# Landmarks loaded onto 128 partitions, a casting load ahead of the identity, and a written-out order for every engine

## The chip, the cores and the metric

The kernel runs on one core of a Trainium2 chip. The metric is the device time of one execution in microseconds. Before the change the median of three runs is 244.42 us (243.48 to 244.64).

## The reference

Eight batches of landmark attention with eight heads are followed by a two-layer network with a smooth ReLU. Each head has 576 tokens of 64 elements and 32 landmarks `p`; the network takes 4608 tokens of 512 elements through 2048 hidden ones.

```python
def sm_attn(qq, kk, vv):
    s = scale * np.matmul(qq, kk.transpose(0, 1, 3, 2))
    a = np.exp(s - np.max(s, axis=-1, keepdims=True))
    a = a / (np.sum(a, axis=-1, keepdims=True) + 1e-09)
    return np.matmul(a, vv)
p_packed = sm_attn(p, k, v)
out = sm_attn(q, p_packed, p_packed)          # 8 x 8 x 576 x 64
x = out.transpose(0, 2, 1, 3).reshape(4608, 512)
h = x @ w_in                                  # 512 x 2048
g = np.where(h >= 1, h, np.where(h <= -1, 0, (h + 1) ** 2 / 4))
return g @ w_out                              # 2048 x 512
```

## The kernel before

**Per batch.** The keys and queries are turned so that the head's 64 elements lie on partitions: by TensorE (PE) for batches 0 and 1 (`tp`, L471), by transposing transfers on SyncE's queue (SP) for the others (L500). The scores of landmarks against keys (`sp`, L528) go through ScalarE's (ACT) exponential (`ex`, L533); their product with the values is `pk` (L624, L619), cast into `ppT`. The scores of queries against landmarks (`s`, L700) give `eT` (L723); its sums (`sm`, L728), their logarithm and its negative exponential (`ln`, `rc`) and one product on VectorE (DVE) give `A` (L742). The values meet `w_in` first: `mp` (L686) is `ppT` times a quarter of `w_in`, cast into `M` (L271). The hidden layer is then `h` = `M` times `A` (L814), in 16 pieces of 128 hidden elements. Each piece goes through `x` on ACT (L820), `t` on DVE or ACT (L828, L830) and a product into `hT` on DVE (L835). The second layer takes 16 products per 128 tokens into `o` (L889); `o` is copied to `ob` and stored.

**Landmarks.** `pT` holds them turned, `[64 twice, batch, g, a, x, 32]`. Before, `p_raw` and `p_nat` hold the landmark number on 32 partitions, two batches loaded by one transfer each on SP's and ACT's queues (L395); the rest (`p_late`) by six casting loads of GpSimd (L375). PE turns them against the identity (L426, L421) and four copies per group write `pT`.

**Loads.** GpSimd (POOL) issues the casting loads, float32 to bfloat16, in one queue: k, v and q of batch 0, the quarters of `w_in` and `w_out`, and then batch after batch (`load`, `load_w_in`, `load_w_out`). Half of batch 0's keys comes as float32 over SP's and ACT's queues into `k_raw` (L401) and is cast by DVE and ACT.

**What sets the order.** Every step is a `Task` with its engines, costs, dependences and buffers. `Plan.run` is a list scheduler with a model of the two kinds of queues: at each moment it takes the ready step that can start first, by a rank where several can. The ranks come from the table `AT`, `HID`, `OUT` (two numbers per batch and stage). Steps are emitted in the order of their starts, so each engine's queue is in that order. The gaps that the plan leaves on PE before the first `o` are filled with products of a tile of zeros (`warm`, L942). Where a step may run on DVE or ACT, the plan chooses.

```python
w, o, kT, x, t, ob = 3, 2, 2, 4, 4, 4      # buffers that matter; w and o are in PSUM
LOADS = "k0 v0 q0 win0 win1 wout0 k1 win2 win3 wout1 v1 wout2 q1 wout3 v2 q2 p k2"
```

Of the kernel before, what the change touches and what calls it, by code (L numbers as in the profile page):

```python
# [11 lines left out]
class Task:  # L12
# [4 lines left out]
    def __init__(self, rank, ways, deps=(), takes=(), mode=None, behind=()):  # L17
        self.rank, self.ways, self.deps = rank, ways, list(deps)
        self.behind = [d for d in behind if d is not None]
        self.takes, self.frees, self.mode = list(takes), [], mode  # L20
        self.start = self.end = self.engine = None
        self.users = []


class Plan:
# [8 lines left out]
    CLAIM = 0.3  # L34
# [4 lines left out]
    def __init__(self, buffers):  # L39
# [8 lines left out]
    def add(self, rank, ways, deps=(), takes=(), mode=None, behind=()):  # L48
        t = Task(rank, ways, deps, takes, mode, behind)
        self.tasks.append(t)  # L50
        return t
# [38 lines left out]
    def run(self, slack):  # L90
# [7 lines left out]
        ready = [t for t in self.tasks if not waiting[id(t)]]  # L98
        done = []

        def served(users):
            for u in users:
                waiting[id(u)] -= 1
                if waiting[id(u)] == 0:
                    ready.append(u)

        def finished(t):
# [5 lines left out]
            served(t.users)  # L113

        while len(done) < len(self.tasks):
            best = None
            found = defaultdict(list)
            left = {b: sorted(v) for b, v in self.slots.items()}
            for t in sorted(ready, key=lambda t: t.rank):
                at = max((d.end + self.LATENCY for d in t.deps), default=0.0)  # L120
                at = max([at] + [d.start + 0.001 for d in t.behind])
                need = defaultdict(int)
                for b in t.takes:
                    need[b] += 1
                short = any(len(left[b]) < n for b, n in need.items())
                wants = at < self.free["PE"] + self.CLAIM
                for b, n in need.items():
                    if not short:
                        at = max(at, left[b][n - 1] + self.LATENCY)
                    if wants:  # L130
                        del left[b][:n]
                if short:
                    continue
                for e in t.ways:
                    if e == "SP" and self.held is not None:
                        continue
                    start = max(self.free[e], at)
                    if e == "PE" and self.mode is not None and t.mode != self.mode:
                        start = max(start, self.free[e] + self.SWITCH)
                    found[e].append((start, t))  # L140
            for e, some in found.items():
                first = min(x[0] for x in some)
                at, t = min((x for x in some if x[0] <= first + slack.get(e, 0.0)), key=lambda x: (x[1].rank, x[0]))
                if best is None or at < best[0]:
                    best = at, t, e
# [5 lines left out]
            assert best is not None, "no step can take its buffers"  # L151
            at, t, e = best
            if e == "PE" and t.mode != self.mode:
                at = max(at, self.free[e] + self.SWITCH)
            ready.remove(t)
            keep, lasts = t.ways[e][:2]
            t.start, t.engine, t.end = at, e, at + lasts
# [6 lines left out]
            served(started[id(t)])  # L164
# [19 lines left out]
def kernel(  # L184
# [20 lines left out]
    P = 128  # L205
# [17 lines left out]
    SPLIT, AHALF, WPARTS, MPARTS, QLATE, ORDER3, ORDER = 2, 1, 1, 0, 1, 0, 2  # L223
# [3 lines left out]
    L1 = 15.967  # L227
    AT = [dict(kT=148.161, qT=275.48, sc=149.063, pk=-49.085, s2=-3.905, sm=-182.602, M=178.569, **{"M+": -129.863}),
          dict(kT=-39.644, qT=-48.123, sc=-66.351, pk=124.743, s2=170.079, sm=-187.478, M=-105.149, **{"M+": 146.812}),
          dict(kT=115.732, qT=51.477, sc=130.42, pk=237.931, s2=-181.084, sm=-29.758, M=169.369, **{"M+": -44.412}),  # L230
          dict(kT=29.446, qT=-25.092, sc=52.472, pk=243.839, s2=179.754, sm=-32.11, M=115.586, **{"M+": -71.343}),
          dict(kT=38.536, qT=86.402, sc=153.04, pk=258.796, s2=-13.152, sm=-43.327, M=-95.344, **{"M+": 110.184}),
          dict(kT=1.864, qT=113.754, sc=282.551, pk=400.409, s2=-26.009, sm=-92.874, M=125.845, **{"M+": 0.958}),
          dict(kT=126.633, qT=239.492, sc=-4.526, pk=382.024, s2=-90.437, sm=32.434, M=177.14, **{"M+": -62.453}),
          dict(kT=27.261, qT=148.76, sc=40.741, pk=216.362, s2=-45.985, sm=130.271, M=1.019, **{"M+": -201.613})]
    HID = [(27.4, 1.3921), (-10.054, 2.601), (22.49, 3.9747), (126.895, 4.8485), (231.121, 9.6612), (-18.141, 4.6461), (3.622, 15.8949), (451.41, 5.8147)]
    OUT = [[(235.954, -183.0), (268.544, -106.533), (35.947, 20.528), (122.624, -48.891)],
# [24 lines left out]
    plan = Plan(dict(BUFS, dma=8, exn=1))  # L262
# [28 lines left out]
    p_raw = work.tile([NP, 2, H, D], f32, tag="vv", name="p_raw", bufs=BUFS["vv"])  # L291
    p_nat = work.tile([NP, 2, H, D], bf16, tag="ln", name="p_nat", bufs=BUFS["ln"])
# [22 lines left out]
    consts = plan.add(-1000, {"DVE": (2.4, 2.4, constants)})  # L315

    identity = plan.add(-998.5, {"POOL": (0.6, 1.25, lambda e: make_identity(nc, ident))})
# [3 lines left out]
    last_of = {"loads": identity}  # L321
# [8 lines left out]
    def dma(key, rank, emit, mb, takes=(), settle=0.9):  # L330
        t = plan.add(rank, {"DMA": (0.78, 2.1, emit, mb / 0.405, settle)}, takes=list(takes) + ["dma"])
        plan.release("dma", [t])
        chain("loads", t)
# [14 lines left out]
    def load(nm, b, rank):  # L348
# [629 lines left out]
```

## Time and profile before

| | us |
|---|---|
| median of three runs | 244.42 (243.48 to 244.64) |
| span of the profiled execution, first to last instruction | 241.1 |
| median less span | 3.3 |
| PE busy | 233.3 |
| ACT busy | 192.7 |
| DVE busy | 177.6 |
| POOL busy | 31.4 |
| granted TensorE clock, mean | 1.000 |

The profiled execution has no time of its own beside its span; the median of the runs stands for it. One row of a profile's group or timeline names the line, engine, operation and tiles (written <- read), then a count and times. Times in the timeline count from the span's start. "Idle" is the time in which the engine stood before an instruction, with what ended it in brackets.

### The profile page before, as it was taken

To read this page: it belongs to the slowest core of one execution; us is meant where nothing else is said; L and a number is where in the kernel's file an instruction comes from. 1 tells how busy PE (TensorE), PEld (TensorE's weight loads), DVE (VectorE), ACT (ScalarE), POOL (GpSimd) and SP (SyncE) were. 2 spreads that over 40 slices of the span, in tenths; PEclk is the share of its full clock that TensorE was granted. 3 is DMA by queue.
4 is the path that set the end of the run, shared out by engine and by line. 5 is a ranking of instruction groups with operands and counts; after the bars stand their busy time and mean duration, and the time that the engine had idled before them with its cause. 6 is when DMAs were issued, how large, how long until landed. Compare 5 with 4: busy or idle time off the path is not lost.

```text
span 241.1 us, 5370 instructions
## 1 busy us (share of the span) xinstructions
PE 233.3 (97%) x2117; PEld 133.9 (56%) x2154; DVE 177.6 (74%) x311; ACT 192.7 (80%) x342; POOL 31.4 (13%) x47
## 2 busy tenths in 40 slices
PE   8999999999999999999999999999999999999995
PEld 2646555466554665466645564465546644565454
DVE  4549997678967998789936898689999955899000
ACT  3779996988969985999776988999789988888111
POOL 8462006200220040030030003000000000000000
PEclk9999999999999999999999999999999999999999
DMA  7999999996999999999999999999930301202233
GB/s 158 196 206 207 206 205 205 197 241 132 125 198 149 234 164 251 152 221 221 194 165 246 233 141 147 161 141 226 191 94 4 85 5 44 71 21 65 65 87 90
DMA packets 64138, 37.03 MB, mean 154 GB/s; under 512 B 36720, under 2 KB 59632, under 8 KB 64112
## 3 DMA queue, kind: packets, MB, share of 16 engines
q0 software_dynamic: 24336, 18.25, 52.6%
q1 hardware_dynamic: 38960, 17.87, 36.7%
q10 hardware_dynamic: 816, 0.56, 0.8%
q8 instruction: 17, 0.28, 0.5%
q14 instruction: 9, 0.07, 0.1%
HBM read 37.22 MB, written 9.44 MB: 194 GB/s over the span
## 4 chain that ended last, share of the span: by engine, by line
PE 81%; DVE 6%; DMA 5%; ACT 4%; POOL 2%; issue 2%; POOLq 0%; ACTq 0%
PE o L889 48%; PE h L814 21%; DMA w_in_sb<-in_moe_w_in_dram 5%; DVE hT L835 4%; PE mp L686 3%; PE pk L619 2%; PE sm L728 1%; DVE t L828 1%; ACT x L820 1%; PE sp L528 1%; PE s L700 1%; ACT t L830 1%; POOL q L352 1%; ACT M L271 1%; PE o L942 1%
## 5 line engine op out<-in xcount | busy, mean ns | idle before, releaser
L889 PE MATMUL o<-w_out_sb,hT 128*128 128x512 bf16 (+2 forms) x574 | 140.9, 367 | 1.9 <-issue 0.6
L835 DVE SCALAR_TENSOR_TENSOR hT<-t 128x576 bf16<-128x576 f32 (+1 forms) x130 | 93.7, 746 | 4.3 <-ACT t L830 2.3
L820 ACT ACTIVATE x<-h 128x576 f32<-128x576 f32 (+1 forms) x130 | 78.6, 651 | 9.1 <-PE h L814 8.5
L889 PEld LDWEIGHTS <-hT 128*128 128x128 bf16 x608 | 55.8, 98 | 49.8 <-issue 6.1
L814 PE MATMUL h<-A,M 128*128 128x288 bf16 x512 | 78.5, 286 | 0.6 <-ACT M L271 0.3
L814 PEld LDWEIGHTS <-M 128*128 128x128 bf16 x512 | 49.9, 98 | 27.6 <-issue 1.1
L830 ACT ACTIVATE t<-x 128x576 f32<-128x576 f32 (+1 forms) x57 | 39.4, 693 | 0.6
L828 DVE TENSOR_SCALAR t<-x 128x576 f32<-128x576 f32 (+1 forms) x73 | 33.3, 456 | 7.1 <-ACT x L820 6.7
L271 ACT COPY ob<-o 128x512 f32<-128x512 f32 (+2 forms) x22 | 12.0, 552 | 17.0 <-PE o L889 16.9
L742 DVE SCALAR_TENSOR_TENSOR A<-eT,rs,rc 128x576 bf16<-128x576 bf16 (+1 forms) x18 | 12.8, 748 | 11.5 <-ACT rc L737 11.5
L271 ACT CAST M<-mp 128x1024 bf16<-128x1024 f32 (+1 forms) x20 | 19.1, 992 | 2.7 <-PE mp L686 2.7
L352 POOL DMA_DIRECT2D k<-in_k_dram x8 | 6.7, 843 | 87.8 <-DMA kT<-k 68.4
L271 DVE CAST M<-mp 128x1024 bf16<-128x1024 f32 (+1 forms) x13 | 15.3, 1180 | 3.1 <-PE mp L686 3.1
L271 DVE COPY ob<-o 128x512 f32<-128x512 f32 x16 | 10.8, 688 | 6.9 <-PE o L889 6.9
L723 ACT ACTIVATE eT<-s,rs 128x576 bf16<-128x576 f32 x16 | 11.1, 742 | 2.5 <-PE s L700 2.5
L942 PE MATMUL o<-zeros 128*128 128x512 bf16 (+1 forms) x35 | 10.5, 431 | 1.3 <-DVE zeros L307 1.2
L732 ACT ACTIVATE ln<-sm 128x576 f32<-128x576 f32 x16 | 10.3, 652 | 1.2 <-PE sm L728 0.7
L686 PE MATMUL mp<-w_in_sb,ppT 64*32 64x512 bf16 x256 | 10.9, 380 | 0.2
L271 ACT CAST ppT<-pk 64x128 bf16<-64x128 f32 x24 | 6.2, 260 | 5.7 <-PE pk L634 4.0
L737 ACT ACTIVATE rc<-ln 128x576 f32<-128x576 f32 (+1 forms) x18 | 10.4, 625 | 0.1
L352 POOL DMA_DIRECT2D v<-in_v_dram x8 | 6.2, 779 | 21.9 <-PE pk L624 15.2
L533 ACT ACTIVATE ex<-sp 96x768 bf16<-96x768 f32 (+1 forms) x12 | 8.1, 709 | 0.5 <-PE sp L528 0.4
(59 smaller groups left out, 116.7 us busy)
## 6 DMA issues: line engine op xcount, KB each, us to landing
v<-in_v_dram POOLq DMA_DIRECT2D x8, 576.0 KB, 11.6
out_dram<-ob SPq DMA_DIRECT2D x23, 192.0 KB, 4.5
k<-in_k_dram POOLq DMA_DIRECT2D x7, 576.0 KB, 8.7
q<-in_q_dram POOLq DMA_DIRECT2D x7, 576.0 KB, 12.8
out_dram<-ob SPq DMA_DIRECT2D x24, 128.0 KB, 2.9
w_out_sb<-in_moe_w_out_dram POOLq DMA_DIRECT2D x4, 512.0 KB, 19.7
w_in_sb<-in_moe_w_in_dram POOLq DMA_DIRECT2D x3, 512.0 KB, 15.2
out_dram<-ob SPq DMA_DIRECT2D x23, 64.0 KB, 4.5
```

The costliest lines, as they stand in the source:

```text
L271: i = (nc.vector.tensor_copy if e == "DVE" else nc.scalar.copy)(to, of)
L352: G_.dma_start(tokens(nm, b)[:, heads(hs)], rows_of(nm, b, hs))
L686: m = nc.tensor.matmul(have["mp", b, f][a * NP:(a + 1) * NP, g], have["ppT", b][r, g, a], w_in_sb[r, a, f * FW:(f + 1) * FW], start=True, ...
L723: nc.scalar.activation(have["eT", b, g], have["s2", b, g][:, :, :HALF], AF.Exp, scale=rs_of[b][:, g, 1:])
L742: V.scalar_tensor_tensor(have["A", b][:, g, xs], have["eT", b, g][:, xs], rs_of[b][:, g, :1], have["rc", b, g][:, xs], ALU.mult, ALU.mult)
L814: nc.tensor.matmul(have["h", b, fi][:, hf, :HALF], have["M", b][:, g, fi * P:(fi + 1) * P], have["A", b][:, g, hf], start=(g == 0), stop=( ...
L820: nc.scalar.activation(have["x", b, fi][:, hs[0]:hs[-1] + 1], have["h", b, fi][:, hs[0]:hs[-1] + 1, :HALF], AF.Prelu, bias=-1.0, alpha=0.5)
L828: V.tensor_scalar(t, x, 1.0, 0.0, ALU.add, ALU.max)
L830: nc.scalar.activation(t, x, AF.Relu, bias=1.0)
L835: V.scalar_tensor_tensor(dst, t, 1.0, t, ALU.min, ALU.mult)
L889: nc.tensor.matmul(have["o", key][:, :w], hT[:, fi, i * P:(i + 1) * P], w_out_sb[:, fi, cols], start=(fi == 0), stop=(fi == KF - 1))
L942: nc.tensor.matmul(o[:, :w], zeros[:, :P], zeros[:, :w], start=True, stop=True)
```

## The change

The landmarks lie on 128 partitions: partition 16 h + m holds landmarks 2m and 2m + 1 of head h, 128 elements, so a row read from memory is 512 bytes instead of 256. Batches 0 and 1 come in one transfer on SP's queue (ACT's queue now starts with its half of `k_raw`), batches 2 to 7 in one casting load. PE turns one 128 x 128 square per batch. The copies into `pT` write runs of 16 elements, and for batches 0 and 1 each batch has copies of its own. GpSimd issues two casting loads, the first part of q and half of k of batch 0, before it builds the identity. The plan no longer chooses: a table `ORDER` gives every step its place on its engine (and DVE or ACT by a letter), and `Plan.run` only works out when each step starts, to place the fillers. The order of all engines is written anew by that table, and two memsets that stood early on DVE stand behind the first `A`.

```diff
-        self.rank, self.ways, self.deps = rank, ways, list(deps)
+        self.rank, self.ways, self.deps = float(rank.rstrip("AD")), ways, list(deps)
+        self.engine = next(e for e in ways if len(ways) == 1 or e[0] == rank[-1])
...
-        self.free = defaultdict(float, DMA=1.95)
+        self.free = defaultdict(float, DMA=0.75)
...
+        for t in sorted(self.tasks, key=lambda t: t.rank):
+            lines[t.engine].append(t)
...
+    ORDER = """
+    first 0 0 0 1 5D 4D
+    load 1 2 0 3 4 6 5 7 9 8 10 11 12 13 14 15 16 20 21 19 17 22 18 24 23 25 26 27 28 29 30 31 32 33 34 35
...
-    p_raw = work.tile([NP, 2, H, D], f32, tag="vv", name="p_raw", bufs=BUFS["vv"])
-    p_nat = work.tile([NP, 2, H, D], bf16, tag="ln", name="p_nat", bufs=BUFS["ln"])
+    p_raw = work.tile([P, 2, X * D], f32, tag="vv", name="p_raw", bufs=BUFS["vv"])
+    p_nat = work.tile([P, 2, X * D], bf16, tag="ln", name="p_nat", bufs=BUFS["ln"])
+    p_rows = p.rearrange("b h (m j) d -> (h m) b (j d)", j=X)
...
-    last_of = {"loads": identity}
+    last_of = {}
...
-            have["p"] = work.tile([P, 2, H, D], bf16, tag="vv", name="p_late", bufs=BUFS["vv"])
-            for b in range(2, B):
-                i, r = divmod((b - 2) * NP, P)
-                G_.dma_start(have["p"][r:r + NP, i], p[b].rearrange("h n d -> n h d"))
+            have["p"] = work.tile([P, B - 2, X * D], bf16, tag="vv", name="p_late", bufs=BUFS["vv"])
+            G_.dma_start(have["p"], p_rows[:, 2:])
...
-        for i, queue in enumerate((nc.sync, nc.scalar)):
-            queue.dma_start(p_raw[:, i], p[i].rearrange("h n d -> n h d"))
+        nc.sync.dma_start(p_raw, p_rows[:, :2])
...
+    identity.behind += landed["k", 0, 4]
...
-    def landmarks(b0, b1, rank, deps, behind=()):
+    def landmarks(b0, b1, of, deps):
         def turn(e):
+            have["tpp", b0] = tp = wide([P, b1 - b0, 1024 if b0 == 0 else P], bf16, "tpp")
+            for i in range(b1 - b0):
+                nc.tensor.transpose(tp[:, i, :P], of()[:, i], ident)
...
+        for bs in [range(b, b + 1) for b in range(b0, b1)] if b0 == 0 else [range(b0, b1)]:
+            for j in range(X):
+                    *[(lambda x=x, j=j, bs=bs: pT[x * D:(x + 1) * D, bs[0]:bs[-1] + 1, :, :, x, j * NP // X:(j + 1) * NP // X],
+                       lambda j=j, bs=bs: have["tpp", b0][j * D:(j + 1) * D, bs[0] - b0:bs[-1] + 1 - b0, :P].rearrange(
+                           "p b (a g m) -> p b g a m", a=Q, g=G))
+                      for x in range(X)],
```

More of the change, by code (lines that the diff above doesn't have):

```diff
@@ L150, in run @@
                 continue
-            assert best is not None, "no step can take its buffers"
+            assert best is not None, "the order of an engine waits for itself"
             at, t, e = best
-            if e == "PE" and t.mode != self.mode:
-                at = max(at, self.free[e] + self.SWITCH)
-            ready.remove(t)
+            lines[e].pop()
             keep, lasts = t.ways[e][:2]
-            t.start, t.engine, t.end = at, e, at + lasts
+            t.start, t.end = at, at + lasts
             self.free[e] = at + keep
@@ L163, in run @@
             done.append(t)
-            served(started[id(t)])
+            for u in started[id(t)]:
+                waiting[id(u)] -= 1
             if len(t.ways[e]) > 3:
@@ L921 @@
         first = 0 if b % 2 == 0 else 4
[L922 to L927 removed]
+        for i in range(first, first + 4 + b % 2):
+            output(b // 2, i, (256, 128, 128) if (b, i) == (B - 1, 8) else (d_model,))
+    order = plan.run()
     first_o = min(t.start for t in o_of.values())
```

342 lines of the change are left out of this document (189 added, 153 removed), and 7 rows, old and new, of the table OUT.

## The prediction

> **What bounds the kernel now.** The page comes first: the busy times of the engines, and the chain that ended last by engine.
>
> ```profile
> PE 233.3 (97%) x2117; PEld 133.9 (56%) x2154; DVE 177.6 (74%) x311; ACT 192.7 (80%) x342; POOL 31.4 (13%) x47
> PE 81%; DVE 6%; DMA 5%; ACT 4%; POOL 2%; issue 2%; POOLq 0%; ACTq 0%
> ```
>
> TensorE (PE) sets the time, but 97% hides where it does no useful work, because the kernel fills its early gaps with products of a tile of zeros (L942). So the second view is busy time by stage, for all instructions and then for L942 alone (start:end, length, then PE busy and count, PEld, DVE, ACT, POOL, granted clock, DMA share, GB/s; the L942 row has PE and PEld only).
>
> ```profile
> 0.00:31.50 31.50, 28.84 (x325) 16.12 (x331) 20.94 (x53) 23.44 (x46) 13.60 (x23) 1.00 1.16 195
> 31.50:238.20 206.70, 204.42 (x1792) 117.76 (x1823) 156.69 (x259) 169.03 (x297) 17.81 (x24) 1.00 0.88 149
> 238.20:241.10 2.90, 0.00 (x0) 0.00 (x0) 0.00 (x0) 0.22 (x1) 0.00 (x0) 0.98 0.19 52
> 0.00:31.50 31.50, 10.52 (x35) 3.62 (x38) 1.00 1.16 195
> ```
>
> Up to 31.5 us PE does at most 28.84 - 10.52 = 18.3 us of useful work, so 13.2 us are lost there. In the next 206.7 us only 206.70 - 204.42 = 2.3 us are idle. After that 2.9 us of copy and store remain. A change of order can win in the first 31.5 us, hardly after them.
>
> What sets the pace there is the transfers. The next rows are the stages of the start (same columns).
>
> ```profile
> 1.50:2.00 0.50, 0.50 (x2) 0.15 (x1) 0.40 (x4) 0.50 (x1) 0.50 (x1) 1.00 0.27 66
> 2.00:2.50 0.50, 0.50 (x3) 0.20 (x2) 0.26 (x5) 0.02 (x1) 0.50 (x2) 1.00 1.06 210
> 2.50:3.00 0.50, 0.50 (x3) 0.23 (x2) 0.00 (x0) 0.00 (x0) 0.50 (x1) 1.00 0.75 119
> 3.00:3.50 0.50, 0.50 (x3) 0.18 (x2) 0.29 (x1) 0.00 (x0) 0.50 (x2) 1.00 0.87 243
> 3.50:4.00 0.50, 0.50 (x3) 0.00 (x0) 0.39 (x1) 0.00 (x0) 0.50 (x1) 1.00 0.87 292
> 4.00:5.00 1.00, 1.00 (x10) 0.41 (x10) 0.28 (x1) 0.28 (x1) 1.00 (x3) 1.00 1.10 293
> 5.00:6.00 1.00, 1.00 (x5) 0.46 (x4) 0.49 (x3) 0.46 (x2) 1.00 (x3) 1.00 1.26 190
> 20.00:30.00 10.00, 9.59 (x108) 6.16 (x108) 9.37 (x18) 9.57 (x19) 1.20 (x2) 1.00 1.26 206
> ```
>
> Then the tile view of the last quarter of w_in, and PE's and ACT's timelines around its use (start, length, engine, line).
>
> ```profile
> L363 POOL DMA_DIRECT2D w_in_sb<-in_moe_w_in_dram x1: 750/750/750, 12.7 to 12.7; - x1
> DMA to landing us min/median/max: 17.1/17.1/17.1
> ```
> ```profile
> 29.82 0.41 PE L686 MATMUL mp<-w_in_sb,ppT 64*32 64x512 bf16 x8
> 30.62 0.65 PE L814 MATMUL h<-A,M 128*128 128x288 bf16 x4
> 31.52 0.28 PE L814 MATMUL h<-A,M 128*128 128x288 bf16 x1 [0.25 <-ACT M L271]
> ```
> ```profile
> 30.46 1.01 ACT L271 CAST M<-mp 128x1024 bf16<-128x1024 f32 x1
> ```
>
> The DMA share reaches 1.26 at 5 us and still stands there between 20 and 30 us: one full queue. The last quarter of w_in is issued at 12.7 and lands 17.1 later, at 29.8, and PE uses it at 29.82. In that same stretch DVE (9.37 of 10) and ACT (9.57 of 10) are full too.
>
> **The change, part by part.** Every sum is against the profiled execution, whose span is 241.1 us; the median of the runs is 244.42, so 3.3 us lie around the span and are kept.
>
> *The queue starts earlier (the main term).* Here are the first issues, from the timeline:
>
> ```profile
> 0.74 0.21 POOL masks.py:197 MEMSET ident<- 128x128 bf16 x1 [0.29 <-POOLq L962]
> 0.77 0.42 ACTq L395 DMA_DIRECT2D p_raw<-in_p_dram  x1
> 1.23 0.47 ACTq L401 DMA_DIRECT2D k_raw<-in_k_dram  x1
> 1.48 0.81 POOL L352 DMA_DIRECT2D k<-in_k_dram  x1 [0.17 <-issue]
> 2.28 0.79 POOL L352 DMA_DIRECT2D v<-in_v_dram  x1
> ```
>
> The start of GpSimd's queue before (names are tiles; ident is the identity):
>
> ```order
> masks.py:197 MEMSET ident 128x128
> masks.py:199 ISA
> masks.py:199 AFFINE_SELECT ident<-ident 128x128
> L352 DMA k<-in_k_dram 96x4x384
> L352 DMA v<-in_v_dram 96x8x384
> L352 DMA q<-in_q_dram 96x4x384
> ```
>
> And the same place now:
>
> ```order
> L411 DMA q<-in_q_dram 96x4x384
> L411 DMA k<-in_k_dram 96x4x384
> masks.py:197 MEMSET ident 128x128
> masks.py:199 ISA
> masks.py:199 AFFINE_SELECT ident<-ident 128x128
> L411 DMA v<-in_v_dram 96x8x384
> ```
>
> Two loads pass the identity, and q's first part is ahead of k. The first load goes out at 0.74 instead of 1.48: 0.74 us sooner. The identity, 0.74 us from its start to the first load before, is then done near 0.74 + 2 x 0.81 + 0.74 = 3.1, some two microseconds later than now; only the landmarks' transposes want it so soon. ACT's half of k_raw, with no landmark transfer ahead of it, goes at 0.77, 0.46 us sooner.
>
> How much reaches the end of the queue? The bytes stay the same, so only unused room counts. Against 1.26, the rows from 1.5 to 5.0 leave 0.50 + 0.10 + 0.26 + 0.20 + 0.20 + 0.16 = 1.4, or 1.1 us of full rate, most of it before 4. The 293 GB/s at 4 to 5, and 190 once the share is full, say that the plain float32 loads had the engines until nearly 5 and the casting loads (half the bytes written) came only then, some 3 us after their issue. From 4.2 instead, they find 0.74 x 0.16 / 1.26 = 0.1 us of room; the 0.46 us by which half of the plain traffic is earlier gives about 0.2. That is 0.3; the whole shift would be 0.74; none of it, 0; and no loss, since nothing comes to lie ahead of the queue. I take 0.4, nearer to what the room allows. **-0.4 us (0 to -0.74).**
>
> A page speaks about this gap. The Trainium skill, "DMA: Bandwidth & Descriptors", section "Latency and other measured facts", gives a casting queue's first byte as about 1 us after issue; the 3 us above do not agree with it, and by it the loads would flow from 1.8, where the rows have room, and the term would be the whole -0.74.
>
> *q before k, k1 before w_out.* The reordered loads and their price:
>
> ```profile
> L352 POOL DMA_DIRECT2D q<-in_q_dram x1: 1078/1078/1078, 3.1 to 3.1; - x1
> DMA to landing us min/median/max: 8.6/8.6/8.6
> 10.42 0.84 PEld L624 LDWEIGHTS <-v 96*64 96x64 bf16 x48 [0.46 <-DMA v<-in_v_dram]
> 9.85 0.49 ACT L533 ACTIVATE ex<-sp 96x384 bf16<-96x384 f32 x1 [0.41 <-PE sp L528]
> ```
>
> q's first part landed at 3.1 + 8.6 = 11.7, 1.3 us behind v (10.4, where PE waited for it). Ahead of k and v it delays both by 1.3 - 0.4 = 0.9 us: v to 11.3. k's scores, whose exponentials ended at 10.34, go as far back, so v still hides them; q's transposes then no longer follow, but precede. Nothing is left to pay, unless the two casts of k, both on DVE now, take longer than v's 0.9 us. The fourth quarter of w_in has the same bytes ahead of it as before, so it lands at 29.8 - 0.4 = 29.4. Batch 1's keys change places with w_out's first quarter:
>
> ```profile
> L352 POOL DMA_DIRECT2D k<-in_k_dram x1: 792/792/792, 11.0 to 11.0; - x1
> DMA to landing us min/median/max: 13.7/13.7/13.7
> L352 POOL DMA_DIRECT2D v<-in_v_dram x8 | 6.2, 779 | 21.9 <-PE pk L624 15.2
> ```
>
> The keys landed at 24.7; without 512 KB at 206 GB/s (2.5 us) ahead of them they land at 24.7 - 2.5 - 0.4 = 21.8, and w_out's quarter about as much later as the keys take. PE has h's and the keys' own products to do meanwhile. Later, batch 2's k, q and p pass its v, whose issue stood 15.2 us for PE, and batch 2's transposing transfers pass six stores in SP's queue; all of it is early by many microseconds. **0.**
>
> *The order around that quarter.* ACT before, around the cast of the fourth quarter's product (ex: batch 1's exponentials; x, t: steps of the activation; M: the cast of w_in's products):
>
> ```order
> L533 ACTIVATE ex<-sp 96x12x64
> L830 ACTIVATE t<-x 128x576
> L820 ACTIVATE x<-h 128x576
> L271 CAST M<-mp 128x2x512
> L820 ACTIVATE x<-h 128x576 x3
> ```
>
> ACT now, at the same place:
>
> ```order
> L330 CAST M<-mp 128x2x512
> L582 ACTIVATE ex<-sp 96x12x64
> L867 ACTIVATE x<-h 128x576
> L330 CAST M<-mp 128x2x512
> L867 ACTIVATE x<-h 128x576 x6
> ```
>
> The cast has one step fewer ahead of it (t goes to DVE, the third quarter's cast comes from there), so the 0.25 us that PE stood at 31.52 for it should go. **-0.25 us (0 to -0.25).** It rests on ACT: if the cast comes as late as now, the wait stays.
>
> DVE, from the first scaled probabilities A on, before:
>
> ```order
> L742 SCALAR_TENSOR_TENSOR A<-eT,rs,rc 128x288 x3
> L828 TENSOR_SCALAR t<-x 128x288
> L835 SCALAR_TENSOR_TENSOR hT<-t 128x288
> L828 TENSOR_SCALAR t<-x 128x288
> L835 SCALAR_TENSOR_TENSOR hT<-t 128x288
> ```
>
> And now:
>
> ```order
> L790 SCALAR_TENSOR_TENSOR A<-eT,rs,rc 128x288 x3
> L594 MEMSET exn 128x12x16
> L594 MEMSET pT 128x768
> L875 TENSOR_SCALAR t<-x 128x288 x4
> L882 SCALAR_TENSOR_TENSOR hT<-t 128x288
> L330 COPY kT<-tp 128x4x192
> ```
>
> Two memsets came here from the start, and the first hT stands behind four t.
>
> ```profile
> L546 DVE MEMSET pT<- 128x768 uint32 x1 | 0.7, 698 | 0.1
> L546 DVE MEMSET exn<- 128x192 uint32 x1 | 0.2, 218 | 0.0
> L271 DVE CAST M<-mp 128x1024 bf16<-128x1024 f32 (+1 forms) x13 | 15.3, 1180 | 3.1 <-PE mp L686 3.1
> L830 ACT ACTIVATE t<-x 128x576 f32<-128x576 f32 (+1 forms) x57 | 39.4, 693 | 0.6
> L828 DVE TENSOR_SCALAR t<-x 128x576 f32<-128x576 f32 (+1 forms) x73 | 33.3, 456 | 7.1 <-ACT x L820 6.7
> ```
>
> The memsets are 0.92 us; ACT now casts a whole quarter of M (1.01) ahead of the first x, so DVE would have stood then: **0**, or +0.92 without that cover. Over the program 15 t move from ACT to DVE: 15 x 0.69 off ACT, 15 x 0.46 onto DVE, neither the bound after 31.5: **0**.
>
> *Landmarks.* The late transposes and the loads they need:
>
> ```profile
> L421 PE MATMUL tpp<-ident,p_late x8: 190/210/219, 59.4 to 59.8; 128*128 128x128 bf16 x4, 64*128 64x64 bf16 x4
> L375 POOL DMA_DIRECT2D p_late<-in_p_dram x6: 578/578/578, 39.6 to 43.4; - x6
> ```
>
> Eight become six, about 0.05 us each where PE is full: **-0.1 us.** GpSimd saves five issues of 0.58 us; they ended near 44, fifteen microseconds ahead of use: **0**. The early transposes (eight to two) and the narrower cast lie in the first 5 us, ahead of the transfers that bound: **0**. The copies into pT write runs of 16 elements now and may take longer; they have the same cover.
>
> *The end.* The last three copies go from ACT to DVE; the 2.9 us behind PE's last product may move by a tenth either way: **0**.
>
> Sum: -0.4 - 0.25 - 0.1 = -0.75: a span of 240.35, and 244.42 - 0.75 = **243.7 us**.
>
> **The rivals.**
> - *The casting queue flows only when the plain loads are through* (for it: 293 GB/s until 5 us): the first term is nil, 244.42 - 0.35 = 244.1. Chance 0.20.
> - *The whole shift passes*: -0.74 - 0.25 - 0.1, 243.3. For it: 1.1 us of room; against it: the late casting traffic. The skill's rule above gives this. Chance 0.18.
> - *The order wins more*: half of the 2.3 us that PE idles after 31.5 goes as well, beside the whole shift: 242.2. For it: every engine's row is written anew; against it: such idle is many short gaps between kinds of product. Chance 0.15.
> - *DVE becomes the bound between 19 and 31 us, and it is slower.* Up to the fourth quarter's cast DVE gains 0.92 of memsets and two and a half t from ACT (2.5 x 0.46 = 1.2), and loses one cast of M (1.2): 0.9 net. And a copy of kT, which waits for batch 1's keys, stands ahead of its second hT:
>
> ```profile
> 20.82 0.46 DVE L835 SCALAR_TENSOR_TENSOR hT<-t 128x288 bf16<-128x288 f32 x1
> ```
>
> Keys at 21.8 and half a microsecond of transposes put it at 22.3 instead of 20.82, 1.5 us. DVE had 0.63 us free in 20 to 30. From that on PE stands for hT one to one: 0.9 + 1.5 - 0.6 = 1.8, and the transfers' gain is useless: 244.42 - 0.1 + 1.8 = 246.1. Against it: the memsets fall into a wait, and the products that need hT also need w_out's quarter, which lands later now. Chance 0.14.
>
> **How the numbers follow.** The forecast has 0.33. Half a percent, 1.2 us, is about what a measurement of this kernel can tell. Faster than 243.2: the third rival's 0.15, some 0.08 of the second and 0.05 of the forecast, 0.28. Slower than 245.6: most of the last rival, 0.12. Between: 0.60. The range, 242.2 to 245.2, goes from the third rival to the last one with half its price; it leaves out about 0.2.
>
> **What would show it.** Right: the first casting load at 0.74, the last quarter of w_in landing near 29.4, PE's useful work in the first 31.5 us up by about 0.65, PE idle about 2.3 us afterwards as now. Wrong: that landing still at 29.8 (first rival) or at 29.0 (second); idle after 31.5 clearly under or over 2.3; waits of PE for hT from DVE between 20 and 33 (last rival).

## The result, and the profile after

The changed kernel takes 252.51 us (median of four, 249.51 to 253.95) against 244.19 us for before on the same chip (243.48 to 244.64): the ratio is 1.0279, 95% interval 1.0213 to 1.0345. It is slower; 243.7 was predicted, in a range of 242.2 to 245.2. The ratio is formed from the executions within 1.5% of the fastest alone, two of the changed kernel's four, so it is lower than that of the two medians. The profiled execution took 253.95 us, with a span of 252.1.

The page's busy times and its chain by engine:

```profile
PE 239.6 (95%) x2148; PEld 135.8 (54%) x2148; DVE 180.6 (72%) x333; ACT 186.2 (74%) x324; POOL 28.5 (11%) x42
PE 76%; DMA 10%; ACT 6%; DVE 5%; issue 2%; SPq 0%; DVEq 0%; ACTq 0%
```

PE's part of the chain fell from 81% to 76%, DMA's rose from 5% to 10%. Busy time by stage (columns as in the prediction; the second row is of the products on zeros, L991, alone, with PE and PEld only):

```profile
0.00:31.50 31.50, 28.22 (x321) 15.80 (x322) 18.37 (x55) 20.56 (x43) 15.61 (x26) 1.00 1.16 193
0.00:31.50 31.50, 12.85 (x40) 4.03 (x40) 1.00 1.16 193
31.50:249.50 218.00, 211.42 (x1829) 120.04 (x1827) 162.23 (x280) 165.59 (x282) 12.90 (x16) 0.98 0.87 141
120.00:140.00 20.00, 17.68 (x141) 9.38 (x134) 12.33 (x21) 14.68 (x25) 1.63 (x3) 0.98 1.23 151
140.00:160.00 20.00, 20.00 (x176) 10.01 (x175) 13.02 (x24) 16.74 (x32) 0.77 (x1) 0.93 1.06 179
160.00:180.00 20.00, 17.25 (x133) 10.35 (x132) 14.49 (x25) 14.27 (x28) 0.77 (x1) 0.91 0.87 155
139.40:142.75 3.35, 3.35 (x13) 1.65 (x12) 3.23 (x7) 1.69 (x4) 0.00 (x0) 0.50 1.15 167
173.55:176.90 3.35, 3.35 (x34) 1.73 (x20) 3.32 (x7) 2.71 (x6) 0.00 (x0) 0.50 0.79 229
```

Up to 31.5 us PE does at most 28.22 - 12.85 = 15.4 us of useful work, 2.9 less than before. After 31.5 us PE idles 218.00 - 211.42 = 6.6 us instead of 2.3, 5.1 us of it in two stages, and twice the granted clock is 0.50. PE's waits (engine, operation <- releaser: us in total, times, longest) name the releaser:

```profile
PE o L940 <- ACT ob L330: 2.8, 1, 2.8
PE o L940 <- DVE ob L330: 2.3, 1, 2.3
PE tpp L474 <- DVE p_nat L495: 1.8, 1, 1.8
```

Before, no wait for `ob` stood there, and no wait of PE after the first 2 us was longer than 0.4. The chain of the stretch from 110 to 176 us (start, length, what) says what the copy into `ob` waited for:

```profile
127.19 10.21 DMA out_dram<-ob
137.53 0.70 DVE ob L330
...
164.67 6.84 DMA out_dram<-ob
171.67 0.59 ACT ob L330
172.30 1.02 PE o L940 x4
```

A store in flight for 10.21 us keeps its `ob`. The next copy out of PSUM waits for that buffer, `o`'s two PSUM buffers stay full, and PE stands (it idles); 34 us later the same with a store of 6.84. Both stores stood in SP's queue behind a transposing transfer, the second behind batch 7's of k, the first behind batch 5's of q:

```profile
L549 SPq DMA_TRANSPOSE qT<-q x1: 8642/8642/8642, 117.9 to 117.9; - x1
DMA to landing us min/median/max: 18.1/18.1/18.1
```

Before, batch 5's transpose of q took a third of that:

```profile
L500 SPq DMA_TRANSPOSE qT<-q x1: 3082/3082/3082, 119.9 to 119.9; - x1
DMA to landing us min/median/max: 5.8/5.8/5.8
```

The start does not go as predicted either. GpSimd's timeline, the last two quarters of w_in, and PE's timeline:

```profile
1.30 0.81 POOL L411 DMA_DIRECT2D q<-in_q_dram  x1 [0.86 <-POOLq L1011]
```
```profile
L422 POOL DMA_DIRECT2D w_in_sb<-in_moe_w_in_dram x2: 755/758/760, 12.8 to 13.5; - x2
DMA to landing us min/median/max: 14.5/15.4/16.3
```
```profile
5.27 0.40 PE L474 MATMUL tpp<-ident,p_nat 128*128 128x128 bf16 x2 [1.76 <-DVE p_nat L495]
8.87 0.37 PE L520 MATMUL tp<-ident,k 96*128 96x96 bf16 x2
13.88 0.94 PE L672 MATMUL pk<-ex,v 96*64 96x32 bf16 x48
30.75 0.41 PE L734 MATMUL mp<-w_in_sb,ppT 64*32 64x512 bf16 x8
```

The first load goes out at 1.30, 0.18 us sooner and not 0.74. The last quarter lands at 13.5 + 16.3 = 29.8, as before. PE stands 1.76 us for the landmarks, the first transposes of k come at 8.87 instead of 6.45, and the first product with the values starts at 13.88 instead of 10.42. PE takes the last quarter of w_in at 30.75, 0.9 us after it landed, where before it was taken at 29.82, as it landed.

### The profile page after: what moved, and what is told of

The parts are those of the page before. It is cut to its first block, busy times and chain, and to the rows that moved or that the text cites. A ratio compares the mean times of both kernels' runs of the same rounds, so it can differ in the third digit from the quotient of the medians.

```text
span 252.1 us, 5395 instructions
## 1 busy us (share of the span) xinstructions
PE 239.6 (95%) x2148; PEld 135.8 (54%) x2148; DVE 180.6 (72%) x333; ACT 186.2 (74%) x324; POOL 28.5 (11%) x42
## 4 chain that ended last, share of the span: by engine, by line
PE 76%; DMA 10%; ACT 6%; DVE 5%; issue 2%; SPq 0%; DVEq 0%; ACTq 0%
PE o L940 42%; PE h L861 20%; DMA out_dram<-ob 8%; PE o L991 2%; PE mp L734 2%; PE tp L520 2%; ACT x L867 2%; DMA p_raw<-in_p_dram 2%; PE pk L667 1%; PE sp L577 1%; PE s L748 1%; DVE A L790 1%; PE sm L776 1%; DVE hT L882 1%; ACT t L877 1%
## 5 line engine op out<-in xcount | busy, mean ns | idle before, releaser
L940 PE MATMUL o<-w_out_sb,hT 128*128 128x512 bf16 (+2 forms) x608 | 148.4, 371 | 5.2 <-ACT ob L330 2.8
L861 PE MATMUL h<-A,M 128*128 128x288 bf16 x512 | 80.5, 289 | 0.3 <-DVE M L330 0.3
L875 DVE TENSOR_SCALAR t<-x 128x576 f32<-128x576 f32 (+1 forms) x89 | 38.7, 454 | 15.8 <-ACT x L867 15.1
L330 DVE COPY ob<-o 128x512 f32<-128x512 f32 (+2 forms) x20 | 12.6, 636 | 24.4 <-PE o L940 19.2
L877 ACT ACTIVATE t<-x 128x576 f32<-128x576 f32 x41 | 27.3, 681 | 0.8 <-DVE hT L882 0.5
L330 ACT COPY ob<-o 128x512 f32<-128x512 f32 x18 | 10.4, 586 | 17.9 <-PE o L940 14.3
L330 ACT CAST M<-mp 128x1024 bf16<-128x1024 f32 (+1 forms) x22 | 21.1, 995 | 1.8 <-PE mp L734 1.7
L330 DVE CAST M<-mp 128x1024 bf16<-128x1024 f32 (+1 forms) x11 | 12.9, 1170 | 2.1 <-PE mp L734 2.1
L991 PE MATMUL o<-zeros 128*128 128x512 bf16 (+1 forms) x40 | 12.8, 443 | 1.2 <-DVE zeros L367 1.2
L411 POOL DMA_DIRECT2D q<-in_q_dram x10 | 7.5, 752 | 35.8 <-DMA qT<-q 29.3
```

Source lines behind the costliest of these rows:

```text
L330: i = (nc.vector.tensor_copy if e == "DVE" else nc.scalar.copy)(to, of)
L411: G_.dma_start(tokens(nm, b)[:, heads(hs)], rows_of(nm, b, hs))
L861: nc.tensor.matmul(have["h", b, fi][:, hf, :HALF], have["M", b][:, g, fi * P:(fi + 1) * P], have["A", b][:, g, hf], start=(g == 0), stop=( ...
L875: V.tensor_scalar(t, x, 1.0, 0.0, ALU.add, ALU.max)
L877: nc.scalar.activation(t, x, AF.Relu, bias=1.0)
L940: nc.tensor.matmul(have["o", key][:, :w], hT[:, fi, i * P:(i + 1) * P], w_out_sb[:, fi, cols], start=(fi == 0), stop=(fi == KF - 1))
```

## The experiments

SP's row is what most of them change. In the rows below `k5`, `q5` and `e5` are the transposing transfers of batch 5's k, q and exponentials, `o13` is the store of the fourth 128 tokens of the second pair of batches:

```
before:  o02 o03 o00 o01 k2 q2 k3 o04 q3 o07 o08 o06 o05 k4 q4 o13 o10 o12 k5 q5 o11 o16 o15 o14 o17 e5 k6 q6 o18 e6 o20 k7 o22 q7 o21 e7
changed: o02 k2 q2 o03 o01 k3 o04 q3 o07 o06 k4 o05 o00 o08 o10 q4 k5 o13 q5 o15 o12 o14 e5 k6 o11 q6 o17 e6 k7 o18 q7 o21 o20 o16 o23 o24 e7
```

Medians stand beside the ratio to before on the same chip. Kernels with such stands (stretches in which PE idles for a buffer or for data) scatter by several microseconds from execution to execution.

### Start or order: the new start with the old order

```diff
     ORDER = """
-    first 0 0 0 1 5D 4D
+    first 0D 0 0 1 4D 2A
```
(and so on: every row as the old plan had it)

> The changed kernel with its new start (landmarks on 128 partitions, first casting load ahead of the identity) but with every engine's old order, written into the table; each new copy of pT stands where the old copy stood. Order theory (the slowdown is made by the new order, the start costs at most the 0.85 us by which TensorE was behind at 36 us): 243.8 to 245.2 us, no idle stretch of TensorE over 1 us after 40 us, clock 1.000. Start theory (the late p_raw, landed at 4.90 instead of 3.11, and what follows from it is the cost): 249 to 253 us, with stands at 135 and 169 us as in the changed kernel.

Measured: 244.53 us (243.79 to 245.35), ratio 1.0034 (1.0018 to 1.0051). Its waits of PE:

```profile
PE tpp L475 <- DVE p_nat L496: 1.4, 1, 1.4
...
PE sp L578 <- DMA kT<-k: 0.7, 1, 0.7
```

No wait for `ob` is left. So the order, with its choice of DVE or ACT, makes nearly all of the 8 us; the start about one. The order also makes PE late at the start: here its useful work up to 31.5 us is 27.91 - 10.79 = 17.1 us, between the 18.3 of before and the 15.4 of the changed kernel.

### Buffers alone: seven `ob`

```diff
-    BUFS = dict(..., x=4, t=4, ob=4)
+    BUFS = dict(..., x=4, t=4, ob=7)
```

> The changed kernel with seven output buffers ob instead of four, all orders as they are. Buffer theory (stores behind transposing transfers in SP's queue keep all four ob, the copy out of PSUM waits for one, o's two PSUM buffers stay full, TensorE stands 2.5 and 2.9 us and then runs 3.41 us at half clock, twice): both stands and both half-clock stretches go, 252.5 less about 2 x (2.7 + 1.7) = 243.7 to 246 us. Start theory and engine-order theory (the work's new sharing between DVE and ACT costs it): 250 to 253 us. Casting-load theory (transposes are slow because casting loads run beside them, so data is late, not buffers): 249 to 253 us, with the stands in other places.

Measured: 254.33 us (252.22 to 256.33), ratio 1.0407 (1.0331 to 1.0483). The buffer theory, taken alone, falls. Its waits of PE, and its transpose of batch 5's q:

```profile
PE s L605 <- DMA kT<-k: 3.4, 1, 3.4
PE h L861 <- ACT x L867: 1.6, 2, 1.3
PE pk L667 <- DMA ex<-exn: 1.5, 1, 1.5
```
```profile
L549 SPq DMA_TRANSPOSE qT<-q x1: 8296/8296/8296, 120.1 to 120.1; - x1
DMA to landing us min/median/max: 17.7/17.7/17.7
```

The wait for `ob` is gone as expected; in its place PE stands for transposed data, `kT` and `ex`. The transpose of q is as slow as before the edit, 17.7 us.

### Stores ahead of the transposes

```diff
-k5 o13 q5 o15 o12 o14 e5 k6 o11 q6 o17 e6 k7 o18 q7 o21 o20 o16
+k5 o13 o15 o12 o14 q5 e5 k6 o11 q6 o17 e6 o18 o21 o20 k7 q7 o16
```

> The changed kernel with SP's row alone changed at the two places: the stores of o15, o12 and o14 ahead of batch 5's transposing transfer of q, and the stores of o18, o21 and o20 ahead of batch 7's transposing transfers of k and q. Four ob buffers as before. Buffer theory: the two stands go or fall below 0.5 us, 244 to 247 us; the transposes come later, and if they then are late themselves a new wait for kT or qT shows, up to 249. Start and engine-order theories: 250 to 253 us.

Measured: 263.71 us (260.53 to 264.06), ratio 1.0777 (1.0706 to 1.0848), the slowest of all. PE waits twice for keys:

```profile
PE s L606 <- DMA kT<-k: 9.9, 2, 6.5
```

The stand for `ob` is gone here too, and the transposes, now behind stores whose outputs are not ready, are late themselves: a wait exchanged for a bigger one.

### Fewer buffers under the old order

```diff
-ob=4
+ob=3
```

> The new start with the old order and three output buffers ob instead of four. Buffer theory: with the old order the stores landed up to 13 us after issue at 151 us with no wait, so there is some slack; three buffers should use it up and bring a stand of 1 to 3 us and a half-clock stretch behind it: 246 to 250 us. If ob buffers do not matter: as the old order with four, 243.8 to 245.2 us.

Measured: 252.81 us (251.08 to 254.22), ratio 1.037 (1.0307 to 1.0433). ACT's timeline shows how the lack of a buffer spreads:

```profile
85.35 0.59 ACT L331 COPY ob<-o 128x512 f32<-128x512 f32 x1 [5.28 <-DMA out_dram<-ob]
85.84 0.69 ACT L878 ACTIVATE t<-x 128x576 f32<-128x576 f32 x1
```

A copy that waits for a store stops its whole engine: `t` and `x` queue behind it, and PE stood 5.0 us for `x`. Four buffers are enough for the old order, three are not.

### Transposes beside casting loads: a gate, pairs, and pairs with seven `ob`

In the changed kernel stores stand between `k4` and `q4`. `k4` has landed (98.96) when `q4` is issued (99.40), k's only buffer is free, and the next casting load of k goes out at 99.51, beside `q4`. Before, `q4` was issued at 98.84 right behind `k4`, which landed at 104.33; the load of k went out at 104.89. GpSimd's timeline of the changed kernel, then of before:

```profile
99.51 0.77 POOL L411 DMA_DIRECT2D k<-in_k_dram  x1 [12.72 <-DMA kT<-k]
```
```profile
104.89 0.77 POOL L352 DMA_DIRECT2D k<-in_k_dram  x1 [17.52 <-DMA kT<-k]
```

The gate makes GpSimd wait for qT ahead of that load (`seen` is a tile of one element):

```diff
             def emit(e, hs=hs):
+                if nm == "k" and b > 3:
+                    nc.gpsimd.tensor_copy(seen, have["qT", b - 1][:1, 0, 0, :1])
                 G_.dma_start(tokens(nm, b)[:, heads(hs)], rows_of(nm, b, hs))
```

> The changed kernel with its own orders; GpSimd additionally copies one element of qT of a batch (4 numbers in all, batches 3 to 6) ahead of the casting load of the next batch's k, so that this load and those behind it on GpSimd start only when that batch's transposing transfer of q has landed. Collision theory (with stores between the two transposes of a batch, the transpose of k has landed and freed its buffer when the one of q starts; the next k load then runs beside it, and the one of q took 17.3 and 18.1 us in the changed kernel against 5 to 8.5 where it goes directly behind that of k): q's transposes of batches 4 and 5 take 5 to 9 us, the two stands go, 244 to 248 us. Buffer theory (which fell with seven ob): no change, 250 to 254. If the loads are then too late instead: a stand for kT or vv, above 252.

Measured: 254.67 us (253.85 to 256.1), ratio 1.0436 (1.0395 to 1.0477). The transpose of batch 5's q, and DVE's timeline:

```profile
L552 SPq DMA_TRANSPOSE qT<-q x1: 3338/3338/3338, 124.6 to 124.6; - x1
DMA to landing us min/median/max: 4.9/4.9/4.9
```
```profile
103.82 0.69 DVE L330 COPY ob<-o 128x512 f32<-128x512 f32 x1 [6.31 <-DMA out_dram<-ob]
104.43 0.81 DVE L795 SCALAR_TENSOR_TENSOR A<-eT,rs,rc 128x576 bf16<-128x576 bf16 x1
```

The collision is real: without the load beside it the transpose takes 4.9 us instead of 18.1. Yet nothing is won. DVE now stands 6.31 us for an `ob` near 100 us, with `A` behind it, for which PE waits 4.0. So the collision alone is not the cause either.

Next, each transpose of q directly behind that of k, with four `ob` and with seven:

```diff
-k3 o04 q3 o07 o06 k4 o05 o00 o08 o10 q4 k5 o13 q5 ... k6 o11 q6 ... k7 o18 q7
+k3 q3 o04 o07 o06 k4 q4 o05 o00 o08 o10 k5 q5 o13 ... k6 q6 o11 ... k7 q7 o18
```

> The changed kernel with SP's row alone changed: for batches 3 to 7 the transposing transfer of q stands directly behind that of k, and the stores that stood between follow. Collision theory: q's transposes of batches 4 and 5 take 5 to 9 us instead of 17.3 and 18.1; the exp transpose of batch 5 and kT of batches 6 and 7 come earlier; the stands at 135 and 169 us go; 244 to 248 us. The stores now stand behind two transposes, so a wait for ob is the risk: a stand of 1 to 3 us near 95 to 105 us and 248 to 252 then. Theory that any new order of DVE, ACT and PE costs it whatever SP does: 250 to 254.

Measured with four: 260.14 us (257.88 to 261.81), ratio 1.0623 (1.0568 to 1.0677). The transpose of batch 4's q takes 7.0 us (17.3 before the edit); that of batch 5's is still slow. The stores wait behind both transposes, and DVE stands:

```profile
106.95 0.69 DVE L331 COPY ob<-o 128x512 f32<-128x512 f32 x1 [8.60 <-DMA out_dram<-ob]
```

> As the run with q's transposes directly behind k's, with seven ob as well. Collision theory: the risk of a wait for ob is gone, 243.5 to 247 us. Order-of-the-other-engines theory: 250 to 254.

Measured with seven: 246.05 us (244.88 to 251.74), ratio 1.0072 (1.0036 to 1.0109). Its waits of PE, its transpose of batch 5's q, and one of its stages:

```profile
PE tpp L475 <- DVE p_nat L496: 1.6, 1, 1.6
...
PE h L862 <- ACT x L868: 0.9, 2, 0.5
```
```profile
L550 SPq DMA_TRANSPOSE qT<-q x1: 4102/4102/4102, 119.1 to 119.1; - x1
DMA to landing us min/median/max: 5.9/5.9/5.9
```
```profile
120.00:140.00 20.00, 20.00 (x170) 10.63 (x169) 14.77 (x26) 16.21 (x28) 2.62 (x3) 1.00 1.14 200
```

Neither edit alone helps: seven `ob` measure 1.0407 and the pairs 1.0623, against 1.0279 for the change itself (the interval of the first just touches that of the change). Both together bring the kernel back to 1.0072. The rest of the new order, with its shares of DVE and ACT, is left in place; beside the start, which measures 1.0034 with the old order, it costs some 1 us at most, and the two intervals overlap.

The useful work of PE up to 31.5 us is 28.46 - 13.19 = 15.3 us here, as little as in the changed kernel. So the late start of PE is not what makes the 8 us.

### The gate with seven `ob`, and the pairs with the landmarks on two queues

The first combines two edits shown above; the second adds to the pairs with seven `ob`:

```diff
-        nc.sync.dma_start(p_raw, p_rows[:, :2])
+        for i, queue in enumerate((nc.sync, nc.scalar)):
+            queue.dma_start(p_raw[:, i:i + 1], p_rows[:, i:i + 1])
```

> The changed kernel with both edits of the earlier runs: GpSimd's wait for qT ahead of the next batch's load of k, and seven ob. Two-sided theory (each edit alone only moves the stands: seven ob leave q's transposes beside the loads, the wait leaves the stores behind k's transpose with four ob): no stand over 1 us after 40 us, 244.5 to 247 us, as with q's transposes directly behind k's and seven ob (246.05). If the rest of the new order costs it: 250 us or more.

Measured: 250.59 us (248.7 to 253.85), ratio 1.0227 (1.0189 to 1.0265): better than either edit alone, but not cured. The gate holds back the loads themselves (batch 5's k is loaded at 111.69 us, at 104.31 in the pairs with seven `ob`), and PE stands for a late transpose:

```profile
PE h L866 <- ACT x L872: 2.1, 1, 2.1
PE pk L672 <- DMA ex<-exn: 1.6, 1, 1.6
```

That the late loads make these 2% is argued, not shown. The pairs also let q's transposes go out sooner (batch 4's at 98.46, under the gate at 105.97); how much of their gain is that, and how much the absent collision, no run separates.

> The changed kernel with q's transposes directly behind k's, seven ob, and the landmarks on two queues: the new order with the causes named so far taken out. If nothing else in the new order costs time: 243.3 to 244.5 us, level with before or better by up to 0.5. If the new order of DVE, ACT and PE costs something of its own: 245 to 248.

Measured: 244.99 us (243.51 to 248.54), ratio 1.0066 (1.0029 to 1.0103). The stand for `tpp` is gone, but the ratio hardly moves: between 0.3 and 1% stays.

### The reverse: stores between k4 and q4 under the old order

```diff
-k4 q4 o13 o10 o12 k5 q5
+k4 o13 o10 q4 o12 k5 q5
```

> The new start with the old order (244.5 us), and SP's row changed at one place: the stores of o13 and o10 stand between the transposes of k and q of batch 4, as stores do in the changed kernel. Collision theory: the casting load of k of batch 5 then runs beside q's transpose of batch 4, which takes 12 to 18 us instead of 8.5; what follows is late as in the changed kernel: 247 to 254 us. If the stores between do not matter: 244 to 245.5.

Measured: 244.61 us, ratio 1.0027 (1.0005 to 1.0049), no harm. The trace says why it is no test: the two stores held SP for 2.4 us only, and `k4` was still under way (landed at 106.69) when `q4` went out at 102.87, so the load of k came later all the same, and `q4` took 6.9 us.

### Store order

Before, stores stand in the order of the copies. In the changed kernel they do not: o11, copied at 115.46, is stored at 146.70 behind o14, o16 (125.10) at 174.55. So a third theory was that SP's row itself starves `ob`. First the stores in the order of the copies, then that with pairs; and the reverse under the old order:

```diff
-k4 o05 o00 o08 o10 q4 k5 o13 q5 o15 o12 o14 e5 k6 o11 q6 o17 e6 k7 o18 q7 o21 o20 o16
+k4 o08 o06 o05 o10 q4 k5 o13 q5 o12 o11 o15 e5 k6 o16 q6 o14 e6 k7 o17 q7 o18 o20 o22
```
```diff
-k5 q5 o11 o16 o15 o14 o17 e5 k6 q6 o18 e6 o20 k7 o22 q7 o21
+k5 q5 o15 o14 o17 e5 k6 o11 q6 o18 e6 o20 k7 o22 q7 o16 o21
```

> The changed kernel with four ob and the places of stores and transposes in SP's row as they are; only which output goes to which of the store places is changed, so that stores stand in the order in which their copies into ob stand, as in the kernel before (whose row has exactly that order). Store-order theory (in the changed kernel five of the middle outputs held their ob for 26.7 to 62.4 us, o11 34.6 and o16 52.1, since later outputs' stores stand ahead of theirs; before none was held over 20.4): no ob is held over 21 us, both stands at 135 and 169 us go or fall below 1 us, 245 to 249 us; what stays is q's transposes beside the casting loads. If only the transposes matter: 250 to 254.

Measured: 257.34 us (248.98 to 259.53). They scatter too widely for an interval, and no gain shows. In the profiled one a stand for `ob` remains:

```profile
PE o L941 <- DVE ob L331: 2.2, 1, 2.2
```

> As the run with stores in the order of their copies, and q's transposes directly behind k's for batches 3 to 7; four ob. If store order and collision together are the cause: 244 to 246.5 us, as with q's transposes behind k's and seven ob (246.05), with no ob more than before. If four ob are too few for the new order of outputs in any case: a stand of 1 to 4 us and 248 to 256.

Measured: 260.99 us (256.42 to 263.86), ratio 1.0574 (1.0521 to 1.0627).

> The new start with the old order (244.5 us) and two stores of SP's row moved back as the changed kernel has them: o11's behind the transpose of batch 6's k, o16's behind batch 7's q. Store-order theory: two of four ob are then held 30 to 50 us, TensorE stands 2 to 8 us for o's PSUM and runs at half clock behind it, 249 to 258 us. If store order does not matter: 244 to 245.5.

Measured: 244.42 us (243.84 to 246.39), ratio 1.0058 (1.0028 to 1.0088), as the other runs with the old order. SP's timeline shows the edit at work: o11 goes out at 143.80 and o16 at the start of the second row, 170.22; they were copied at 116.7 and 122.3.

```profile
143.80 1.46 SPq L959 DMA_DIRECT2D out_dram<-ob  x2
170.22 2.28 SPq L959 DMA_DIRECT2D out_dram<-ob  x4
```

The store-order theory falls both ways: mending it does not help the new order, and breaking it does not hurt the old one from 117 us on.

### What the start costs

All four keep the old order; they change the start alone: the landmarks on two queues (diff above), the identity first, both, and the first with more fillers.

```diff
-    identity.behind += landed["k", 0, 4]
+    landed["k", 0, 4][0].behind.append(identity)
```
```diff
-            fill.append((at, n))
+            fill.append((at, n + 4 * (8.0 < at < 12.5)))
```

> The new start with the old order (244.53, 1.0034 of before) and the landmarks of batches 0 and 1 on two queues, a batch each, SP and ACT, ahead of the two halves of k_raw, as before had them. Late-landmark theory (p_raw lands at 4.9 instead of 3.1 because ACT's half of k_raw goes beside it; TensorE stands 1.4 us for it and is granted its full clock at 7.74 instead of 5.46): p_raw lands at 2.9 to 3.4, the stand for tpp goes, 243.5 to 244.1 us. If it is the casting load ahead of the identity instead: 244.3 to 244.8.

Measured: 244.99 us (242.69 to 246.53), ratio 1.0042 (1.0008 to 1.0076). In the profiled execution the stand for the landmarks is gone, but the clock falls to half, after PE had stood 0.35 and 0.57 us near 9 and 10.5:

```profile
12.65:15.95 3.30, 3.08 (x32) 1.93 (x31) 1.34 (x5) 1.62 (x3) 2.48 (x4) 0.50 1.24 206
```

> The new start with the old order, but GpSimd builds the identity ahead of the first casting load again; the landmarks stay in one transfer on 128 partitions. Late-landmark theory: p_raw still lands near 4.9 and TensorE stands over 1 us for it, 244.3 to 245.0 us. If the first casting load ahead of the identity costs it (its packets beside p_raw's): p_raw lands earlier, 243.5 to 244.1.

Measured: 244.81 us, ratio 1.0067 (1.0044 to 1.009).

> The new start with the old order, landmarks on two queues, and 4 half filler matmuls on zeros more at each of the three places between 8 and 12.5 us. The run without them had 242.7 us where the clock stayed full and 244.8 to 246.5 where it fell to half for 3.41 us at 12.6 (0.93 us idle in two pieces at 8.9 to 10.9 ahead of it). Clock theory: the idle pieces are filled, the clock stays full, 242.4 to 243.2 us, below before. If the fillers delay the work behind them instead: 243.5 to 245.

Measured: 243.98 us (243.14 to 246.03), ratio 1.0032 (1.0008 to 1.0057). The clock stays full from 4.5 us on in the profiled execution, yet the kernel is not below before.

> The new start with the old order, the landmarks of batches 0 and 1 on two queues, and the identity ahead of the first casting load: only the shape of the landmarks (128 partitions) and their copies are left of the change. With the load ahead of the identity this was 244.99 us (1.0042). If that load's packets beside k_raw (landed at 5.5 and 6.0) delay the first transposes of k: 243.2 to 243.8, level with before. If the landmark copies or the fixed order as such cost it: 244.3 to 245.5.

Measured: 244.46 us (243.62 to 246.09), ratio 1.0061 (1.0035 to 1.0087).

Seven kernels with the new start and four `ob` in the old order have ratios from 1.0027 to 1.0067, 0.7 to 1.6 us, and neither the late landmarks nor the load ahead of the identity accounts for it, alone or together. What the last of these runs keeps of the change is the landmarks' shape with its four copies into `pT`, and an order and fillers that are fixed. Which of these costs the microsecond stays open.

### The clock behind the stands

```diff
                     if fi == 0:
+                        idle = wide([P, 2 * FW], f32, "idle")
+                        for _ in range(12):
+                            nc.tensor.matmul(idle[:, :FW], zeros[:, :P], zeros, start=True, stop=True)
```
(for o18 and o23 alone)

> The changed kernel with twelve matmuls on zeros (12 x 0.2158 us, into a free PSUM buffer) ahead of the first matmul of o18 and of o23, which are the two that stood 2.5 and 2.9 us for o's PSUM. They do work in the stand only. Clock theory (each stand is followed by 3.41 us at half clock, which costs 1.7 us more): the two half-clock stretches go, the stands stay, 252.5 less 2 x 1.7 = 248.5 to 250 us. If the clock falls for another reason, or the fillers come on top: 252 to 256.

Measured: 253.68 us (249.14 to 255.1), the change itself 252.51 (249.51 to 253.95); no gain can be seen. In the profiled execution the clock is full from 120 to 180 us, but PE stands elsewhere as well:

```profile
PE pk L667 <- DMA ex<-exn: 1.6, 1, 1.6
PE o L944 <- DVE ob L330: 1.6, 1, 1.6
```

So the half clock is not simply an extra 1.7 us per stand. The changed kernel's own executions say the same: one took 253.43 us at a mean granted clock of 1.000, the profiled one 253.95 at 0.986. That a faster PE only comes earlier to the next wait is a likely reason, not a shown one. With these scattered times it is not settled how much of the 8 us the half clock makes.

## Why the prediction was wrong, point by point

- *q before k, k1 before w_out* is the step that failed. It let "batch 2's transposing transfers pass six stores in SP's queue" and priced SP's new row at 0, since all of it was "early by many microseconds". That speaks of batch 2 alone. The row was new for every batch, and what a store behind a transpose costs with four `ob` was not read, though the trace of before has transposes of 4.9 to 13.5 us on that queue. The order measures 6 us by the ratios (1.0279 against 1.0034 with the old order), 7.5 by the medians.
- The same step had "Nothing is left to pay" for q ahead of k, since v, at 11.3, would hide k's scores. v landed at 12.3, but the product with it started only at 13.88: the keys were turned 2.4 us later, and their exponentials ended at 13.77 instead of 10.34. The pairs with seven `ob` have the same late start and end at 1.0072, so this is the smaller miss.
- *What bounds the kernel now* concluded that order "can win in the first 31.5 us, hardly after them". The 2.3 us of idle time after 31.5 bound a gain, not a loss. Nor did the transfers still set the pace up to 31.5: the last quarter lay landed for 0.9 us before PE took it. PE's useful work up to there was to rise by about 0.65 us and fell by 2.9. No rival could lose time after 33 us; the only slower one (DVE) did not come: no wait for `hT` shows.
- *The queue starts earlier*, -0.4: 0. The load went out at 1.30, since GpSimd's sequencer let its first transfer go only then (idle 0.86 before it), 0.56 us later than the memset that stood there. The last quarter landed at 29.8 as before, which is the first rival's sign; with a shift of 0.18 us instead of 0.74 that rival was hardly put to the test.
- *The order around that quarter*, -0.25: the wait for ACT's cast of `M` went as forecast, and no wait of PE shows between 20 and 36 us. It won nothing, since PE itself came 0.9 us later to the product ahead of that cast. (The one wait of the changed kernel for a cast of `M`, 0.27 us, lies at 103.8 us.)
- *Landmarks*, -0.1, with the early ones at 0: PE had to wait for the early ones. One transfer with ACT's half of k_raw beside it landed at 4.90 instead of 3.11, and PE stood 1.76 us. Yet taking that stand away brought no gain that can be told from the spread. The late transposes' 0.1 is too small to be seen.
- *The order*, "neither the bound after 31.5: 0": nothing speaks against it. The `t` moved to DVE (16 by the counts on ACT, 57 and 41; the prediction has 15) are still there in the pairs with seven `ob`, at 1.0072.

The cause, as far as shown: in the new order outputs become due while SP is held by transposes. Either stores stand between two transposes, and the next casting load slows the second one from about 6 to 18 us; or they stand behind both, and four `ob` do not last. With one edit alone stands remain; with the pairs and seven `ob` the kernel is 0.7% above before, and the new start with the old order is 0.3 to 0.7% above it too. (The gate with seven `ob`, 1.0227, cures both as well; that it pays for later loads is argued.) Why four suffice for the old order, even with o11 and o16 held back, stays open. No version has a ratio below 1.

## What to carry to other kernels

A queue served in order is an engine too: a new order must be priced on it row by row, with what each transfer holds (a buffer, and the engine that waits for that buffer) and what it lets start (the next load into the buffer that it frees). Idle time bounds only what a reordering can win; what it can lose is bounded by nothing in the profile of before, so a table that rewrites all rows deserves a wide upper end. Where removing one suspected cause changes nothing, remove two at once before giving either up.

## What the runs showed of the hardware

- A transposing transfer between SBUF tiles took 4.9 and 5.1 us where no casting load was issued during it (the gate), 5.8 where the first was issued 2.7 us into it (before), and 17.3 to 18.4 where two or three were issued between just ahead of it and 6 us into it (the changed kernel, seven `ob`, pairs). The Trainium skill, "DMA: Bandwidth & Descriptors", section "Queues, rings and completion order", says that a DMA engine serves its queues in turn, packet by packet; the slowing here fits that, though no trace shows the packets, and the price is a factor of three and more. Stores behind it in SP's queue landed 9.7 to 10.2 us after their issue, and 2.1 at 181 us, where the queue was empty.
- After PE had stood 2.33 us the granted clock was 0.50 for 3.4 us; with longer trouble it lasted longer: in the pairs with four `ob`, from 104.4 to 114.6:

```profile
104.40:114.60 10.20, 6.11 (x23) 3.32 (x24) 5.24 (x8) 2.68 (x5) 2.35 (x3) 0.50 0.96 194
```

The Trainium skill, "TensorE: Matmul & The Clock Gate", "Part 1: The HAM clock gate", tells of a window of about 3.4 us, and of an idle window ahead of a fall. The length agrees; the stands here, 2.33 and even 0.35 with 0.57 us, were shorter than a window, so in these runs the clock fell without an idle stretch of that length.
